# Sparse attention and gated FFN on one core: few large casting loads on one queue, values in 64-token rows, fewer casts

## The chip, the cores and the metric

One Trainium2 chip, one of its cores. The metric is device time in microseconds (us) of one execution. Most executions of a kernel agree closely; some ran at a lower granted TensorE clock and over 1.5% above the fastest run of their kernel. These are called slow here, and only fast runs enter a ratio. A profile is one execution. Stage times come from one profile per kernel and carry that uncertainty.

The engines: PE is TensorE (matmul), PEld its weight loads, DVE is VectorE, ACT is ScalarE, POOL is GpSimd, SP is SyncE. In the traces below VectorE, GpSimd and the matmuls of TensorE keep program order: where one of them waits, what stands behind it waits too.

## The reference

Attention of 4 batches, 8 heads, 768 tokens, 64 channels, followed by a gated FFN (512 to 1536 to 512). A token sees its neighbours within 15 positions, and 24 blocks of 32 tokens by one summary each (elementwise maximum of the keys, mean of the values).

```python
block, window = (32, 16)
k_sum = k.reshape(B, H, nb, block, D).max(axis=3)
v_sum = v.reshape(B, H, nb, block, D).mean(axis=3)
scores_l = scale * np.matmul(q, k.transpose(0, 1, 3, 2))
mask_l = np.abs(pos[:, None] - pos[None, :]) < window
scores_s = scale * np.einsum('bhsd,bhnd->bhsn', q, k_sum) + np.log(block)
a = softmax(concatenate([where(mask_l, scores_l, -1e9), scores_s]))      # shortened
attn = np.matmul(a, concatenate([v, v_sum]))
x = attn.transpose(0, 2, 1, 3).reshape(B * S, H * D)
return (1 / (1 + np.exp(-(x @ w_gate))) * (x @ w_val)) @ w_out
```

## The kernel before

For each tile of 64 queries the kernel multiplies one 120-row operand: 96 near tokens (64 and a halo of 16 on each side) and 24 block means. The values of a batch lie in one of two buffers `vx_t[0]`, `vx_t[1]`; batches alternate between them. Every part of these buffers that no load fills is set once, at the top of the program, ahead of all loads:

```python
vx_t = [const.tile([128, NQ, H, 66], BF16, name=f"vx{i}") for i in range(2)]
...
for t_ in vx_t:
    nc.vector.memset(t_[0:16, 0], 0.0)              # no token before the first
    nc.vector.memset(t_[64:96, NQ - 1], 0.0)
    nc.vector.memset(t_[:, :, :, 64:66], 1.0)       # the column that sums the weights
```

Values come through GpSimd's queue in one casting load (f32 in memory, bf16 in SBUF) per tile of 64 queries. Keys and queries of batches 0 and 1 come plain through the queues of SyncE and ScalarE and are cast by an engine. The opening, in program order:

```python
sk = [load_qk(k, 0, p, ...) for p in range(NP)]                     # SyncE queue
sq = [load_qk(q, 0, p, st, half=0, queue=nc.scalar) ...]            # ScalarE queue
load_v(0, 0, 3); make_masks(); load_v(0, 3, 6); make_zband(); load_v(0, 6, NQ)
for f0, nf in ((0, 1), (1, 1), (2, 2), (4, 2), (6, 2), (8, 2), (10, 2)):
    for wb, wap in ((wg_bf, moe_w_gate), (wv_bf, moe_w_val)):
        load_w(wb, wap, f0, nf)                                     # GpSimd queue
...                                                                 # attention of batch 0, first half
# q second half, w_out, keys and queries of batch 1 (cast on GpSimd), values of batch 1
```

The FFN works on half a batch (384 tokens) and one of 12 slices f of the hidden width at a time. The two products of an f, gate and value, come from one pool of four buffers.

```python
def m1(self, f, hf, c0=0, c1=NP):
    ...
    gp, vp = ps(...), ps(...)                        # four buffers in all
    # four matmuls into gp (gate), four into vp (value)
    nc.scalar.activation(out=gate, in_=gp, func=ACT.Tanh, scale=0.5)
    nc.vector.scalar_tensor_tensor(                  # hT, VectorE
        out=self.hT[hf][:, f, :], in0=gate, scalar=1.0, in1=vp, op0=ALU.add, op1=ALU.mult)
```

The softmax here doesn't subtract the row's maximum and nothing guards it: scores larger than these inputs give would overflow.

## Time and profile before

| | before |
|---|---|
| time, median of 3 runs | 255.56 us (253.16 to 256.45) |
| span of the profiled execution | 251.1 us |
| TensorE busy | 230.2 us, 92% |
| first full group of the FFN starts | 28.1 us |
| second half of batch 0's FFN starts | 49.5 us |

The page's slices cut the span in 40 parts; a digit is the busy share in tenths. A timeline lists start, length, engine, line and operation, and in brackets how long the engine had been idle and which event ended that. The lines of this page are shown in the prediction below. Busy time by stretch: the columns are the stretch, its length, then busy time and count of PE, PEld, DVE, ACT and POOL, then granted TensorE clock (1.00 is full), DMA share and GB/s.

```profile
28.10:49.50 21.40, 18.71 (x211) 11.36 (x209) 10.82 (x23) 12.04 (x24) 11.86 (x17) 1.00 1.22 270
```

This is the first half of batch 0's FFN: TensorE is busy for 18.71 of its 21.40 us, and the missing 2.69 are the wait for weights that the prediction shows.

### The profile page before, as it was taken

The page shows a single profiled execution, that of the slowest core. Times are in us where ns is not written, and L with a number is a line of the kernel's source. Part 1 is how long each engine was busy: PE and PEld are TensorE (multiplying, and loading weights), DVE is VectorE, ACT ScalarE, POOL GpSimd, SP SyncE. Part 2 cuts the span into 40 slices and gives each one's busy share as a digit, 9 for nine tenths or more (in the row PEclk, how much of TensorE's full clock was granted, in tenths as well). Part 3 has the DMA queues.
Part 4 walks back from the last instruction along what each step waited for, and adds up shares of the span by engine and source line. Part 5 has one row for each costly group of instructions (what it writes and reads, how often), then busy time and mean ns, then how long its engine had stood idle before and what let it go on. Part 6 is the DMA issues. An engine that isn't in the chain of part 4 may idle for free.

```text
span 251.1 us, 5090 instructions
## 1 busy us (share of the span) xinstructions
PE 230.2 (92%) x2020; PEld 130.3 (52%) x2032; DVE 119.2 (47%) x243; ACT 107.8 (43%) x193; POOL 111.7 (45%) x151
## 2 busy tenths in 40 slices
PE   1696899599999999799999999999999999999993
PEld 1473566366544556455554455555544465655441
DVE  5876348247833412976563208766543034444000
ACT  2862476239943344445631134645511243333121
POOL 8998276489998389994069930000000000000000
PEclk9999999999999999999999999999999999999999
DMA  6999999999999999999999965600024310000122
GB/s 220 238 158 162 226 270 287 263 189 142 124 122 170 225 221 145 193 171 206 176 121 163 197 171 132 113 13 3 0 76 147 117 42 0 4 0 0 57 112 84
DMA packets 100687, 34.27 MB, mean 136 GB/s; under 512 B 84496, under 2 KB 97208, under 8 KB 100280
## 3 DMA queue, kind: packets, MB, share of 16 engines
q0 software_dynamic: 70720, 12.46, 65.7%
q1 hardware_dynamic: 28856, 20.70, 33.5%
q10 hardware_dynamic: 1088, 0.79, 1.0%
q8 instruction: 16, 0.26, 0.4%
q14 instruction: 7, 0.06, 0.1%
HBM read 34.34 MB, written 6.29 MB: 162 GB/s over the span
## 4 chain that ended last, share of the span: by engine, by line
PE 71%; DMA 17%; POOL 6%; issue 2%; DVE 1%; ACT 1%; SPq 0%; POOLq 0%; ACTq 0%; DVEq 0%
PE m L414 22%; PE gp L397 21%; PE vp L397 21%; DMA wv<-in_moe_w_val_dram 11%; POOL vx L166 3%; DMA kTn<-nat 3%; PE sc L257 2%; PE av L340 2%; DMA vx<-vx 2%; PE vsp L280 1%; PE tp L197 1%; POOL wg L174 1%; DVE kTx L233 1%; PE br L368 1%; POOL wv L174 1%
## 5 line engine op out<-in xcount | busy, mean ns | idle before, releaser
L405 DVE SCALAR_TENSOR_TENSOR hT<-gate,vp 128x384 bf16<-128x384 f32 x96 | 52.8, 551 | 68.9 <-PE vp L397 65.0
L397 PE MATMUL vp<-xT,wv 128*128 128x384 bf16 x384 | 78.6, 326 | 4.2 <-DMA wv<-in_moe_w_val_dram 2.7
L397 PE MATMUL gp<-xT,wg 128*128 128x384 bf16 x384 | 78.8, 327 | 1.1 <-ACT xT L371 1.1
L404 ACT ACTIVATE gate<-gp 128x384 f32<-128x384 f32 x96 | 47.4, 494 | 51.4 <-DVE hT L405 42.9
L414 PE MATMUL m<-wo,hT 128*128 128x512 bf16 x276 | 64.3, 379 | 0.6
L397 PEld LDWEIGHTS <-wv 128*128 128x128 bf16 x384 | 37.5, 98 | 30.6 <-issue 3.1
L397 PEld LDWEIGHTS <-wg 128*128 128x128 bf16 x384 | 35.3, 98 | 22.1
L414 PEld LDWEIGHTS <-hT 128*128 128x128 bf16 x288 | 26.9, 98 | 30.7
L166 POOL DMA_DIRECT2D vx<-in_v_dram x48 | 37.0, 800 | 13.1 <-PE sc L257 9.0
L419 ACT ACTIVATE ot<-m 128x512 f32<-128x512 f32 x24 | 14.3, 597 | 52.1 <-PE m L414 51.9
L263 ACT ACTIVATE P<-sc 128x768 bf16<-128x768 f32 x32 | 26.0, 815 | 12.3 <-PE sc L257 12.2
L264 DVE TENSOR_TENSOR P<-P,mask 128x768 bf16<-128x768 bf16 x32 | 17.8, 555 | 14.1 <-ACT P L263 13.9
L311 POOL TENSOR_TENSOR vm<-vm 96x1024 f32<-96x1024 f32 (+4 forms) x20 | 20.4, 1020 | 5.8 <-DMA vm<-in_v_dram 4.4
L233 DVE TENSOR_REDUCE kTx<-kTn 128x24 bf16<-128x768 bf16 x16 | 15.2, 949 | 4.5 <-ACT kTn L203 2.5
L349 DVE TENSOR_TENSOR xs<-av,rec 128x768 bf16<-128x768 f32 (+1 forms) x20 | 15.9, 797 | 0.7
L197 PE MATMUL tp<-ident,qkbf 128*128 128x128 bf16 x96 | 8.9, 253 | 6.9 <-DVE qkbf L120 5.9
L257 PEld LDWEIGHTS <-kTx 64*128 64x128 bf16 x384 | 7.9, 97 | 11.8 <-issue 8.5
L347 DVE RECIPROCAL rec<-av 128x12 f32<-128x12 f32 (+1 forms) x20 | 4.3, 215 | 19.9 <-PE av L340 19.8
L257 PE MATMUL sc<-qT,kTx 64*128 64x64 bf16 x384 | 12.0, 196 | 1.9 <-DVE kTx L237 1.2
L156 POOL DMA_DIRECT2D nat<-in_q_dram x16 | 13.2, 894 | 0.4 <-issue 0.4
L122 POOL CAST qkbf<-nat 128x768 bf16<-128x768 f32 (+1 forms) x12 | 8.5, 723 | 11.0 <-DMA nat<-in_q_dram 7.6
L156 POOL DMA_DIRECT2D nat<-in_k_dram x16 | 13.3, 852 | 0.1
(50 smaller groups left out, 114.0 us busy)
## 6 DMA issues: line engine op xcount, KB each, us to landing
out_dram<-ot SPq DMA_DIRECT2D x24, 256.0 KB, 4.6
vx<-in_v_dram POOLq DMA_DIRECT2D x40, 96.0 KB, 5.4
vm<-in_v_dram SPq DMA_DIRECT2D x4, 768.0 KB
vm<-in_k_dram SPq DMA_DIRECT2D x4, 384.0 KB, 6.9
nat<-in_k_dram SPq DMA_DIRECT2D x4, 384.0 KB
nat<-in_q_dram SPq DMA_DIRECT2D x4, 384.0 KB, 13.9
wo<-in_moe_w_out_dram POOLq DMA_DIRECT2D x6, 256.0 KB, 16.2
nat<-in_k_dram POOLq DMA_DIRECT2D x16, 96.0 KB, 4.2
```

What stands on the lines that cost most here:

```text
L156: nc.gpsimd.dma_start(out=nat[:, h // 2, :, 64 * (h % 2):64 * (h % 2) + 64], in_=tap[b, h].rearrange("(c p) d -> p c d", p=128))
L166: nc.gpsimd.dma_start(out=vx_t[b % 2][r0:r0 + hi - lo, t, :, 0:64], in_=v[b, :, lo:hi, :].transpose([1, 0, 2]))
L233: nc.vector.tensor_reduce(out=kTx[:, 0, W:KX], in_=kTn[:, 16:16 + S].rearrange("p (n w) -> p n w", w=32), axis=AX.X, op=ALU.max)
L257: nc.tensor.matmul(out=sc[:, i, QT * t6:QT * (t6 + 1)], lhsT=kTx[64 * i:64 * i + 64, t, :], rhs=qT[64 * i:64 * i + 64, QT * t:QT * (t + 1) ...
L263: nc.scalar.activation(out=Ph, in_=sc[:, :, 0:6 * QT], func=ACT.Exp, scale=SCALE)
L264: nc.vector.tensor_tensor(out=Ph, in0=Ph, in1=mask[:, None, 6 * hf:6 * hf + 6, :].rearrange("p i t w -> p i (t w)") .to_broadcast([128, 2, ...
L311: nc.gpsimd.tensor_tensor(out=st[:, 0:n], in0=st[:, 0:n], in1=st[:, n:2 * n], op=ALU.add)
L349: nc.vector.tensor_tensor(out=xs[:, 0:3 * G].rearrange("p (g a) i d -> p g (a i) d", g=G), in0=avf[:, :, :, 0:64], in1=rec[:, 0:G].to_broa ...
L397: nc.tensor.matmul(out=o, lhsT=wb[:, c, 128 * f:128 * (f + 1)], rhs=self.xT[:, c, HALF * hf:HALF * (hf + 1)], start=(c == 0), stop=(c == N ...
L404: nc.scalar.activation(out=gate, in_=gp, func=ACT.Tanh, scale=0.5)
L405: nc.vector.scalar_tensor_tensor(out=self.hT[hf][:, f, :], in0=gate, scalar=1.0, in1=vp, op0=ALU.add, op1=ALU.mult)
L414: nc.tensor.matmul(out=self.m3, lhsT=self.hT[hf][:, f, 128 * tt:128 * (tt + 1)], rhs=wo_bf[:, f], start=(f == 0), stop=(f == NF - 1))
```

## The change

Its intent is to get batch 0's inputs and the weights in sooner, and to relieve engines of casts: few large casting loads, all on GpSimd's queue in one order; values in rows of 64 tokens, so that nothing is loaded twice, with VectorE copying the halo of 32 rows; no engine casts for batches 0 and 1; in the opening masks added through a matmul instead of multiplied in; in the opening near and mean products apart; later both halves of a score tile issued together. The core of the diff, cut (the rest is layout, masks and slot tables):

```diff
-    vx_t = [const.tile([128, NQ, H, 66], BF16, name=f"vx{i}") for i in range(2)]
+    vx_t = [const.tile([128, NU + 1, 66], BF16, name=f"vx{i}") for i in range(2)]
...
-    for t_ in vx_t:
-        nc.vector.memset(t_[0:16, 0], 0.0)
-        nc.vector.memset(t_[64:96, NQ - 1], 0.0)
-        nc.vector.memset(t_[:, :, :, 64:66], 1.0)
+    def clear_values(i):
+        t_ = vx_t[i]
+        nc.vector.memset(t_[0:W, :, 64:66], 1.0)
+        nc.vector.memset(t_[W:128, :, 64:66], 32.0)
+        nc.vector.memset(t_[0:16, 0, 0:64], 0.0)
...
+    def load_v(b, u0, u1, r0=0, r1=64):
+        nc.gpsimd.dma_start(
+            out=vx_t[b % 2][r0:r1, u0:u1, 0:64],
+            in_=rows_of(v[b, 0, 0:1], (QT * u0 - 16 + r0) * D, [[D, r1 - r0], [QT * D, u1 - u0], [1, D]]))
+    def load_values(b):
+        if b + 1 < B:
+            load_v(b, 0, NU + 1)
...
+        def halo(self, h0, h1, t0, t1):
+            nc.vector.tensor_copy(
+                out=self.heads(h0, h1, t0, t1, self.vx[64:96, 0:NU]),
+                in_=self.heads(h0, h1, t0, t1, self.vx[0:32, 1:NU + 1]))
...
+        def G(self, g, h=None):                      # block sums of batch 1, VectorE
+            nc.vector.tensor_reduce(out=sm, in_=st.rearrange("p (w d) -> p d w", w=32), axis=AX.X, op=ALU.add)
...
+    load_rows(k, 0, ...), load_rows(q, 0, ...)       # batch 0 (calls shortened)
+    load_v(0, 0, 1, 16, 64)
+    for p in range(NP):
+        load_v(0, 24 * p + 1, 24 * p + 25)
+    load_gates(...)                                  # all of gate and value weights
+    for h in (0, 4):
+        load_rows(k, 1, h, 4, 0, S, k1[:, h:h + 4])
+        load_rows(q, 1, h, 4, 0, S, q1[:, h:h + 4])
+    load_wo(0, 4)
+    load_wo(4, 4)
+    for g in range(2):
+        a1.L(g, queue=nc.gpsimd)
+    load_wo(8, 4)
+    load_values(1)
+    clear_keys(0)
...                                                  # masks, then attention of batch 0, first half
     f0.m1(0, 0, 3, 4)
+    more_masks()
+    clear_values(1)
...
+    NEXT = """
+        3 T0   4 T1   5 Z0   6 T2   7 Z1   8 T3   10 Z2   12 Z3 G0 M0   13 G1 M1   14 H0 H1   16 B0 B1
+        17 A0 A1   18 A2 A3 X0   19 X1   20 X2   21 X3"""
```

In the slot tables a number is a slot of the FFN and the letters are pieces of attention issued after it: T transposes, Q those of the second half's queries, E the key copies of that half, S scores of a half, Z of both, G or R block sums on VectorE or GpSimd, M their scaling and the move into the value buffer, H halo, B spread of the means, A value products, X output transposes.

## The prediction

> **What bounds the kernel now.** I read the page's busy rows first, then the slices, then the chain of waits in order of time, then the timelines of single engines.
>
> ```profile
> PE 230.2 (92%) x2020; PEld 130.3 (52%) x2032; DVE 119.2 (47%) x243; ACT 107.8 (43%) x193; POOL 111.7 (45%) x151
> ...
> PE   1696899599999999799999999999999999999993
> ...
> DMA  6999999999999999999999965600024310000122
> ```
>
> TensorE is the bound: 92% busy, and full from slice 9 on. Whatever is to be won lies in the first eight slices (50 us), in the slot after the last matmul, and in matmul work taken away. There the DMA row reads 9. The chain, in order of time, names what holds the opening (start us, length us, what):
>
> ```profile
> 13.72 0.74 POOL vx L166
> ...
> 25.31 21.82 DMA wv<-in_moe_w_val_dram
> ...
> 47.18 0.82 PE vp L397 x4
> ```
>
> and TensorE's timeline shows the one long pause of the FFN, with its releaser in brackets:
>
> ```profile
> 43.66 0.82 PE L397 MATMUL gp<-xT,wg 128*128 128x384 bf16 x4
> 47.18 0.82 PE L397 MATMUL vp<-xT,wv 128*128 128x384 bf16 x4 [2.69 <-DMA wv<-in_moe_w_val_dram]
> ```
>
> So the opening waits for transfers: values until 18.1 us (the block sums start then), the last weights until 47.1 us. The first half of the first FFN ends at 49.6 us by the chain. The rates, from busy time by stretch (last two columns DMA share and GB/s, which count the bytes written):
>
> ```profile
> 10.00:16.00 6.00, 5.39 (x66) 4.62 (x65) 5.29 (x11) 5.32 (x10) 5.72 (x9) 1.00 2.41 154
> ...
> 20.00:27.00 7.00, 4.51 (x69) 2.55 (x68) 4.84 (x13) 2.02 (x6) 4.91 (x7) 1.00 1.33 171
> ...
> 50.00:54.00 4.00, 4.00 (x26) 2.40 (x25) 1.76 (x4) 1.47 (x3) 3.12 (x5) 1.00 1.24 205
> ```
>
> The first is values alone (rows of 64 bf16), the second gate and value weights, the third the output weights: casting loads write 154, 171 and 205 GB/s, the more the longer the row.
>
> **What the Trainium skill says.** "DMA: Bandwidth & Descriptors", Specifications, gives about 358 GB/s of HBM for one core; a casting load reads twice what it writes, so 171 is 342 read (agrees), 205 is 410 (the trace is above it). The same page, "Issuing engines are not separate DMA queues": all transfers share 16 DMA engines; so moving batch 0's loads from the SP and ACT queues to GpSimd's gains no bandwidth. "TensorE: Matmul & The Clock Gate", Part 1, says that the VectorE queue is strict first in, first out; the trace agrees: the mask copies of 6.88 us stand behind two casts that waited for their loads, 0.86 us for the second, though they needed neither. "VectorE: DVE Perf Modes", the tier table, gives copies of bf16 in SBUF 4 elements a cycle: the 128x1152 key copy takes 0.45 us, which is that rate plus 0.15 us.
>
> **The change, part by part.**
>
> Casts go. Four pairs of key and query casts (0.55 us VectorE, 0.51 ScalarE) and 12 GpSimd casts leave; only the first 8 lay on the opening's path, some 0.5 us per pair. Against it, keys now come by the GpSimd queue: there the first packet moved only about 4.5 us after the first issue (the first value load, issued at 1.55 us, had done nothing by 6 us), while the plain loads had keys for a cast at 4.61 us. Even.
>
> Products. Block sums of batch 0 come by head pair (52 matmuls of 128 columns, not 12 of 512: 2.7 us, now pipelined with the value loads). Those of batch 1 go to VectorE and save 2.7 us of TensorE. Batch 1's transposes double in count (48 more at 55 ns: 2.6 us, or none if pairs overlap). Bias products add 8 x 0.16 = 1.3 us, but only in an opening that waits. Joined score halves save some 12 switches at 0.11 us (a group of four that follows a score group takes 0.76 us, else 0.65): 1.3 us.
>
> Values. A batch needs 64 x 97 rows, not about 96 x 96: a third fewer. The halo becomes two VectorE copies of 32x3168 per batch (825 ns at 4 a cycle + 0.15 = 1.0 us each), the spread of means two of 24x2904 (0.9 us): 3.8 us per batch, beside hT copies of 0.55 us in every 1.30 us. VectorE has room (47%), but in some slots it lags: 1 to 2 us per batch, 3 us in all.
>
> One GpSimd queue, in order, now carries everything. By bytes written and the rates above (keys and queries, 768-byte rows, between 171 and 205, taken as 190): keys and half the queries 1.18 MB, 6.2 us; values 0.79 MB at 154, 5.1; gate and value weights 3.15 MB at 171, 18.4; the other query half 0.39 MB, 2.3. From a first packet at 5 us the weights are in at 37.0 us, not 47.1. Ten microseconds: this is the gain that the change is made for. Behind them: keys and queries of batch 1, 1.57 MB, 8.3 us; output weights 1.57 MB at 205, 7.7; batch 1's values in f32 for the block sums, 1.57 MB, 7.9 us alone at about 0.2 MB a us but partly beside others, taken as 6; batch 1's values in bf16, 5.2. **These last land at 37.0 + 8.3 + 7.7 + 6 + 5.2 = 64 us.**
>
> Now the line that decides. The opening ends with clear_values(1), on VectorE, just before the FFN proper. Its third memset zeroes partitions 0 to 15 of unit 0 of the values of batch 1. The load of batch 1's values was issued earlier in the program and, unlike batch 0's, writes these very bytes (it starts at row 0, as there is a token before). A write after a write to the same bytes must wait. I built two instructions of no kernel to see it: a memset beside a load's columns carries no wait, one on its bytes waits for the load. VectorE runs in order, so from some 22 us, after hT of the first f, it stands until 64 us, and every hT stands behind it. The product tiles have four buffers, two pairs; TensorE can do f = 1 and 2, the gate product of f = 3, and stops at its value product at about 25 us. An idle of some 39 us, in place of a 2.7 us wait. Before, nothing like it: the memsets were put ahead of all loads.
>
> **The sum.** VectorE resumes at 64 us, hT takes 0.55, so the value product of f = 3 starts at 64.6. In the kernel before it started at 31.39 and the span ended at 251.08: 219.7 us of path. From these go the weight wait 2.7, batch 1's block sums 2.7, two query transposes already done in the idle 0.7, switches 1.3; to them come transposes 2.0, a colder TensorE clock after the idle 1.5 (its first transposes here took 0.11 us against 0.055 later), VectorE lag 3. That is 218.8, and a span of 283.4. Time stood 4.5 above span before (255.56 against 251.08): **288 us**, 13% slower.
>
> **Rivals.**
> First, no stall: if the memset waited for nothing, the weights at 37 us would end the first FFN half near 39.5 instead of 49.6; with 2.7 less of sums and 2 more of transposes the span is 241, the time 245, 4% faster. For it: the intent, and the DMA queue as today's limit. Against it: program order and the overlap of bytes, both plain in the source.
> Second, a wait for the same load elsewhere: without the memset, batch 1's halo copies and value products still need a load that lands at 64 us. But they come after the second half of the FFN, at about 61 to 67 us; a few us at most, inside the first rival: 247 to 250.
> Third, VectorE becomes the bound. It has 3.8 us more per batch, and block sums of batch 1 (two reductions of 96x2048, 1 element a cycle, 2.2 us each). For it: joined score halves give it bursts. Against it: over 50% idle now, 65 us of it waiting for value products. Up to 8 us: 293.
> Fourth, the queue is slower or faster than summed. At the skill's 358 GB/s the 20.4 MB read up to there take 57 us, landing 62; at this trace's 410, 50 and 55. If block rows and long descriptors hold up the ring, 70. So 279 to 294.
>
> **Range and chances.** The landing is worth -7 to +6, the work after it -4 to +5, mostly independent. 8 in 10: 279 to 297 us. The stall follows from the source; that I misread it, or that it is harmless, gets 7%, most of which is the first rival. Faster 0.05, same 0.02, slower 0.93.
>
> **What would show each step.** VectorE idle in one piece from about 22 to 64 us, its first instruction after it a memset of 16 partitions released by the DMA of batch 1's values. TensorE empty in the same time (five or six slices near 0), then full to the end. The chain of waits should hold one DMA item of some 39 us, by the name of the values, and gate and value weights should be gone from it. DMA should stay at 9 up to 64 us: weights in by 37, output weights by 53. After 65 us TensorE should need about 219 us to the end. I am wrong if that first memset waits for nothing, if the values land before 50 us, or if FFN stages after it run over 55 us a batch, for then VectorE was the bound.

## The result

| | before | after |
|---|---|---|
| time, median | 255.0 us of 4 runs (253.16 to 256.45) | 291.01 us of 4 runs (289.87 to 292.2) |
| ratio of fast runs | | 1.142, 95% interval 1.1328 to 1.1513 |
| span of the profiled execution | 251.1 us | 289.5 us |

A ratio is the mean time of one kernel's fast runs over that of the other's of the same rounds, so it is not quite the ratio of the medians. The predicted time was 288 us, its range 279 to 297: the change is slower by 14%, where 13% was predicted.

The page of the changed kernel, busy time and slices of 7.2 us:

```profile
PE 237.8 (82%) x2180; PEld 135.8 (47%) x2180; DVE 139.4 (48%) x270; ACT 106.9 (37%) x190; POOL 85.0 (29%) x102
...
PE   1989920003999999399999899999999999999994
...
DVE  6552200004964878951789853068974403444100
...
PEclk9965885555799999779999999999999999999999
DMA  6999999999909000275999999853000740000122
```

Slices 6 to 9 have three zeros of TensorE and four of VectorE (up to 65 us), while the DMA row reads 9: the engines stand, and a transfer runs. VectorE's timeline says which instruction stands, and TensorE's what that does:

```profile
33.68 0.22 DVE L91 MEMSET vx<- 96x194 bf16 x1
34.00 0.22 DVE L92 MEMSET vx<- 32x194 bf16 x1
68.63 0.09 DVE L93 MEMSET vx<- 16x32 uint32 x1 [34.40 <-DMA vx<-in_v_dram]
69.10 1.49 DVE L470 SCALAR_TENSOR_TENSOR hT<-gate,vp 128x384 bf16<-128x384 f32 x3 [0.39 <-issue]
```

```profile
32.11 0.81 PE L462 MATMUL gp<-xT,wg 128*128 128x384 bf16 x4
...
33.41 0.81 PE L462 MATMUL gp<-xT,wg 128*128 128x384 bf16 x4
...
35.26 0.82 PE L462 MATMUL gp<-xT,wg 128*128 128x384 bf16 x4
...
37.12 0.82 PE L462 MATMUL gp<-xT,wg 128*128 128x384 bf16 x4
69.71 1.44 PE L462 MATMUL vp<-xT,wv 128*128 128x384 bf16 x4 [31.77 <-DVE hT L470]
```

The three memsets are the three lines of `clear_values(1)`. The first two touch the columns 64 and 65 only and run at once. The third zeroes 16 partitions of the first 64 channels, which batch 1's load, issued earlier, also writes; it takes 0.09 us and is preceded by 34.40 us of nothing. Behind it stand the `hT` instructions from f = 1 on, and behind those TensorE, for 31.77 us. The four gate products shown are those of f = 1 to 4, so the value product at 69.71 us is that of f = 4. (The prediction, and the expectation of e1_order, call it f = 3.) The waits view adds up the same (engine, line, what it waited for: total, times, longest):

```profile
DVE vx L93 <- DMA vx<-in_v_dram: 34.4, 1, 34.4
PE vp L462 <- DVE hT L470: 32.5, 2, 31.8
```

The chain of waits is less helpful here. It has the idle as one item, but does not name the transfer:

```profile
34.22 34.39 issue
69.71 1.44 PE vp L462 x4
...
110.95 7.07 DVE sm L381 x2
118.06 1.91 DVE vx L324 x2
120.00 0.92 DVE vx L391
120.97 1.48 PE av L408 x24
```

A reader who looks at the chain alone sees "issue" and might look for slow dispatch. The memset's bracket in the timeline, or the waits view, gives the releaser. The last four items are a second place where VectorE now sets the end, at batch 1's values; it comes back below.

### The profile page after: what moved, and what is told of

Its sections match the earlier page's. It is cut to its first block, busy times and chain, and to the rows that moved or that the text cites. A ratio compares the mean times of both kernels' runs of the same rounds, so it can differ in the third digit from the quotient of the medians.

```text
span 289.5 us, 5322 instructions
## 1 busy us (share of the span) xinstructions
PE 237.8 (82%) x2180; PEld 135.8 (47%) x2180; DVE 139.4 (48%) x270; ACT 106.9 (37%) x190; POOL 85.0 (29%) x102
## 4 chain that ended last, share of the span: by engine, by line
PE 64%; issue 15%; DVE 12%; DMA 3%; ACT 3%; POOL 1%; SPq 1%; DVEq 0%; ACTq 0%; POOLq 0%
PE m L479 20%; PE vp L462 17%; PE gp L462 17%; PE av L408 3%; DVE hT L470 3%; DVE sm L381 2%; PE tp L203 2%; DVE P L288 2%; PE sc L280 2%; DMA k<-in_k_dram 2%; DMA kTn<-nat 2%; PE vsp L308 2%; DVE vx L324 1%; PE br L435 1%; ACT P L286 1%
## 5 line engine op out<-in xcount | busy, mean ns | idle before, releaser
L462 PE MATMUL vp<-xT,wv 128*128 128x384 bf16 x384 | 80.5, 332 | 32.5 <-DVE hT L470 32.5
L470 DVE SCALAR_TENSOR_TENSOR hT<-gate,vp 128x384 bf16<-128x384 f32 x96 | 51.9, 552 | 62.6 <-PE vp L462 60.1
L462 PE MATMUL gp<-xT,wg 128*128 128x384 bf16 x384 | 80.5, 331 | 1.2 <-ACT xT L438 0.6
L479 PE MATMUL m<-wo,hT 128*128 128x512 bf16 x288 | 65.8, 384 | 0.0
L479 PEld LDWEIGHTS <-hT 128*128 128x128 bf16 x288 | 27.8, 99 | 32.1 <-issue 1.1
L286 ACT ACTIVATE P<-sc 128x768 bf16<-128x768 f32 x32 | 24.5, 812 | 10.6 <-PE sc L280 10.6
L374 POOL TENSOR_TENSOR vm<-vm 96x1024 f32<-96x1024 f32 (+4 forms) x20 | 20.8, 1040 | 13.7 <-DMA vm<-in_v_dram 12.4
L288 DVE TENSOR_TENSOR P<-P,mask 128x768 bf16<-128x768 bf16 x28 | 16.9, 622 | 5.5 <-ACT P L286 4.4
L151 POOL DMA_DIRECT2D nat<-in_q_dram x16 | 14.6, 914 | 14.0 <-DMA vx<-in_v_dram 5.5
L158 POOL DMA_DIRECT2D vx<-in_v_dram x9 | 12.7, 1426 | 10.1 <-PE br L435 7.5
L417 DVE TENSOR_TENSOR xs<-av,rec 128x768 bf16<-128x768 f32 (+1 forms) x16 | 13.7, 858 | 0.7 <-DVE rec L415 0.2
L438 ACT COPY xT<-br 128x384 bf16<-128x384 bf16 (+1 forms) x12 | 6.9, 585 | 18.8 <-PE br L435 18.8
L408 PE MATMUL av<-vx,P 120*64 120x65 bf16 x336 | 8.4, 210 | 5.2 <-DVE vx L324 3.5
L408 PEld LDWEIGHTS <-P 120*64 120x64 bf16 x336 | 7.2, 124 | 9.2 <-issue 4.1
```

Of the source, the lines that this page charges most:

```text
L151: nc.gpsimd.dma_start(out=nat[:, h // 2, :, 64 * (h % 2):64 * (h % 2) + 64], in_=tap[b, h].rearrange("(c p) d -> p c d", p=128))
L286: nc.scalar.activation(out=Ph, in_=sc[:, :, 0:6 * QT], func=ACT.Exp, scale=SCALE)
L288: nc.vector.tensor_tensor(out=Ph, in0=Ph, in1=mask[:, None, 6 * hf:6 * hf + 6, :].rearrange("p i t w -> p i (t w)") .to_broadcast([128, 2, ...
L374: nc.gpsimd.tensor_tensor(out=st[:, 0:n], in0=st[:, 0:n], in1=st[:, n:2 * n], op=ALU.add)
L408: nc.tensor.matmul(out=av[r:r + 64, t // 6, (t % 6) // 2, i, 0:65], lhsT=P[0:KX, i, t, :], rhs=vx[0:KX, NQ * (2 * p + i) + t, 0:65], start ...
L417: nc.vector.tensor_tensor(out=xs[:, 0:3 * G].rearrange("p (g a) i d -> p g (a i) d", g=G), in0=avf[:, :, :, 0:64], in1=rec[:, 0:G].to_broa ...
```

## The experiments

All twelve runs gave correct results. **Theory**: the third memset waits for the last transfer on the queue, VectorE stands behind it, and that is the whole loss. **Rivals**: without that wait the kernel is faster than before, since weights come earlier (the first rival of the prediction, 245 us); or another wait for the same load, or VectorE, takes its place (the second and third). In the expectations "the base" is the kernel of e1_order. The stages of each kernel, read from the TensorE timeline of one profile, in us from the start:

| kernel | f=1 starts | second half starts | FFN batch 1 | batch 2 | batch 3 | span | profile's state |
|---|---|---|---|---|---|---|---|
| before | 28.1 | 49.5 | 94.0 | 148.0 | 200.3 | 251.1 | fast |
| after | 32.1 | 85.8 | 134.3 | 187.3 | 238.5 | 289.5 | fast |
| e1_order | 30.9 | 54.9 | 102.6 | 156.9 | 208.2 | 259.1 | slow |
| e2_nozero | 32.5 | 54.5 | 102.4 | 156.6 | 207.9 | 258.8 | fast |
| e3_early_load | 27.5 | 68.2 | 116.8 | 170.4 | 221.7 | 272.6 | fast |
| e4_sums_pool | 31.8 | 56.4 | 110.2 | 164.9 | 216.1 | 267.1 | slow |
| e5_warm | 28.8 | 49.2 | 100.7 | 155.6 | 206.9 | 257.8 | fast |
| e6_rest | 32.1 | 54.1 | 102.5 | 157.1 | 208.4 | 259.3 | fast |
| e7_sums_early | 32.4 | 54.1 | 99.6 | 157.5 | 208.8 | 259.7 | slow |
| e8_all | 32.4 | 52.3 | 93.3 | 151.2 | 202.5 | 253.4 | fast |
| e9_queue | 34.1 | 53.1 | 94.2 | 154.8 | 206.1 | 257.0 | slow |
| e10_again | 28.0 | 46.7 | 91.1 | 158.6 | 210.8 | 261.4 | unknown |
| e11_tensor_sums | 28.6 | 47.7 | 92.0 | 147.3 | 198.6 | 249.1 | fast |

### e1_order: the memsets of batch 1 ahead of its load

```diff
     load_wo(8, 4)
+    clear_values(1)
     load_values(1)
...
     more_masks()
-    clear_values(1)
```

> The changed kernel with the same work, one line moved: the memsets of batch 1's value buffer stand ahead of its load in the program. Theory (VectorE stood 34.4 us in order behind one memset that had to wait for the load): the wait is gone, the value product of f = 3 starts near 38 us instead of 69.7, the colder clock just after the idle goes too (some 2 us), so about 34 us less: 257 us, no better than the 255 of the kernel before. Rival (the halo copies and value products of batch 1 need that load anyway, so the wait only moves): at least 280 us, with a wait for the values of batch 1 elsewhere.

Measured 260.32 us median (256.59 to 260.87), ratio 1.018 to the kernel before (1.0091 to 1.0269, two fast runs). The 34-us wait is gone, and so are some 31 us. One moved line is worth almost all of the loss, but the kernel does not come out faster than before.

### e2_nozero: the third memset for batch 0 only

```diff
-        nc.vector.memset(t_[0:16, 0, 0:64], 0.0)
+        if i == 0:
+            nc.vector.memset(t_[0:16, 0, 0:64], 0.0)
```

> The changed kernel with only the third memset left out for batch 1's buffer (0.09 us of work; the result stays right, the load writes those bytes). Theory: as with the line moved, 257 us within 1%. If the two other memsets of that call, which stay where they were, also waited for the load, this would stay near 291 us and the moved line alone would help.

Measured 261.54 us median (260.61 to 264.46), ratio 1.033 (1.0261 to 1.0399). That is more than the 257 us within 1% that were expected, but far from the 291 of the rival. Here nothing else moves: the other two memsets stay behind the load in program order. VectorE in this kernel:

```profile
34.12 0.22 DVE L92 MEMSET vx<- 32x194 bf16 x1
35.33 0.56 DVE L471 SCALAR_TENSOR_TENSOR hT<-gate,vp 128x384 bf16<-128x384 f32 x1 [1.00 <-PE vp L463]
```

So it is not `clear_values` as such, nor its place after the load, but the 16 partitions of shared bytes alone. Zeroing them is needed for batch 0, whose load leaves these rows out; batch 1's load fills them.

### e3_early_load: the wait kept, its transfer moved forward

```diff
+    load_values(1)
     load_wo(0, 4)
     load_wo(4, 4)
     for g in range(2):
         a1.L(g, queue=nc.gpsimd)
     load_wo(8, 4)
-    load_values(1)
```

> The changed kernel with the memset left where it is and the load of batch 1's values moved ahead of the output weights and the block rows in the queue. Theory (the idle lasts until that load lands, wherever it stands in the queue): keys and queries of batch 1 were in at 44.5 us, the values take 5.2 us more, so VectorE resumes near 50 instead of 68.6 us: about 272 us. Rival (the idle lasts until the whole queue is drained, or has to do with the other loads): stays near 291 us.

Measured 274.7 us median (272.84 to 275.37), ratio 1.0817 (1.0771 to 1.0864). The memset's own view, first of the changed kernel and then of this one (duration min/median/max in ns, first and last start; below it what ended the idle):

```profile
L93 DVE MEMSET vx<- x2: 85/85/85, 6.6 to 68.6; 16x32 uint32 x2
...
  DMA vx<-in_v_dram: 34.4, 1
```

```profile
L93 DVE MEMSET vx<- x2: 85/85/85, 6.6 to 51.9; 16x32 uint32 x2
...
  DMA vx<-in_v_dram: 22.3, 1
```

The load lands 16.7 us earlier (51.9 against 68.6) and the span is 16.9 us shorter (272.6 against 289.5): one for one. The end hangs on that landing. This also settles how the prediction could be right without getting the start of the stall right.

### e4_sums_pool: block sums of batch 1 back on GpSimd (with e1_order)

The stage from the second half to batch 1's FFN takes about 48 us in after, e1_order and e2_nozero, against 44.5 before. In the changed kernel TensorE waits there for VectorE:

```profile
110.87 7.16 DVE L381 TENSOR_REDUCE sm<-vm 96x64 f32<-96x2048 f32 x2
```

```profile
119.09 0.25 PE L408 MATMUL av<-vx,P 120*64 120x65 bf16 x2 [3.53 <-DVE vx L324]
120.97 1.48 PE L408 MATMUL av<-vx,P 120*64 120x65 bf16 x46 [1.62 <-DVE vx L391]
```

Two block sums at 3.58 us each hold the halo copies (L324) and these hold the value products. The edit takes the sums from VectorE:

```diff
-    NEXT = "... 12 Z3 G0 M0   13 G1 M1   14 H0 H1   16 B0 B1 ..."
+    NEXT = "... 12 Z3 R0 M0   13 R1 M1   14 H0 H1   16 B0 B1 ..."
```

> As the run with the line moved, and batch 1's block sums on GpSimd (ten additions) instead of two reductions on VectorE. In the changed kernel these took 3.5 us each (7.1 together), the halo and mean copies stood behind them, and TensorE was empty from 115.5 to 121.0 us but for two products, then ran 5 us at half clock. Theory: some 5 to 7 us less than with the line moved alone, 250 to 252 us. Rival (the stage waits for something else there, such as the transfers of the means, or VectorE was not what held it): within 1 us of it.

Measured 268.54 us median (263.71 to 268.84), with one fast run only (263.71), so no ratio. A miss. GpSimd in this kernel (a slow profile):

```profile
69.12 0.82 POOL L151 DMA_DIRECT2D nat<-in_q_dram  x1 [5.77 <-DMA vx<-in_v_dram]
...
76.61 2.28 POOL L158 DMA_DIRECT2D vx<-in_v_dram  x1
78.84 5.97 POOL L374 TENSOR_TENSOR vm<-vm 96x1024 f32<-96x1024 f32 x5
```

GpSimd takes its instructions in order too. The 17 load issues for batch 2 stand ahead of the sums in the program, each issue waits its turn on the transfers, and the sums cannot start before 78.84 us. The stage grew to 53.8 us.

### e5_warm: filler matmuls in the opening (with e1_order)

In the changed kernel's opening the TensorE clock fell to half from 17.3 to 30.9 us. Some more small matmuls of no use are put between the block sums:

```diff
     a0.S(2, 0, True)
+    a0.warm(a0.vsp[:, 256:384], 16)
...
-    a0.sums(1)            # and sums(2, 4), sums(3, 4)
+    a0.sums(1, 6)         # and sums(2, 8), sums(3, 8)
```

> The run with the line moved (the base), and more filler matmuls in the opening: 16 in the 1.3 us in which TensorE waits after the third score group, 6, 8 and 8 ahead of the block sums. In the base and in the changed kernel the granted clock fell to half from 17 or 18 us for 14 us, and the first FFN group came at 30.9 to 32.5 us; in the run with the early load, of the same opening, it happened not to fall there, and the group came at 27.5. Theory (the clock falls as the opening's small matmuls leave TensorE too idle, and this costs 3 to 5 us): the clock stays full, the group comes at 27.5 to 28.5 us, and the time falls by 3 to 4 us against the base. Rival (the opening is set by the landings of the values and the hops between engines, the clock only follows): no gain, or the fillers' own 1 to 2 us lost.

Measured 260.78 us median (259.61 to 261.8), ratio 1.0274 (1.0231 to 1.0317): no gain. The stretch from 14 to 29 us in the kernel before, the changed kernel and this one:

```profile
14.00:29.00 15.00, 11.36 (x144) 7.18 (x143) 8.24 (x22) 5.71 (x13) 10.91 (x15) 1.00 1.60 176
```

```profile
14.00:29.00 15.00, 13.38 (x187) 10.03 (x185) 5.63 (x14) 4.79 (x10) 8.96 (x12) 0.61 2.23 175
```

```profile
14.00:29.00 15.00, 13.11 (x248) 9.53 (x243) 6.83 (x18) 6.24 (x14) 8.98 (x12) 1.00 2.21 174
```

The clock stayed full, the second half started at 49.2 us instead of some 54.7, and then the gain was lost in the next stage, which took 51.5 us instead of 48. Its VectorE:

```profile
74.34 7.18 DVE L381 TENSOR_REDUCE sm<-vm 96x64 f32<-96x2048 f32 x2
...
86.53 0.91 DVE L391 COPY vx<-vx 24x2904 bf16<-24x2904 bf16 x1 [3.08 <-DMA vx<-mb]
89.04 0.91 DVE L391 COPY vx<-vx 24x2904 bf16<-24x2904 bf16 x1 [1.60 <-DMA vx<-mb]
```

After the same two sums, the copies that spread the means waited for the small transfers that bring them; TensorE stood 7.6 us there and its clock was half from 82 to 92 us. The second limit swallows what the first gives.

### e6_rest: the second score halves issued apart (on the changed kernel with e1_order)

```diff
-        1 Q0 Q1   2 E0 E1 Q2 Q3   3 S0b S1b   4 E2 E3   5 S2b S3b
+        1 Q0 Q1 E0 E1   2 Q2 Q3 E2 E3   3 S0b   4 S1b   5 S2b   6 S3b
```

The key copies (E) also come one or two slots earlier.

> The base, with the second half of batch 0's attention spread: keys spread two slots earlier, score halves one per slot and not two. In the base this stage took 24.0 us from the first FFN group to the second half of the FFN, against 18.7 in the kernel before without its weight wait; TensorE stood 2.6 us behind a key copy on VectorE, with two masks, a halo copy and an hT ahead of it, and the clock then fell for 3.4 us. Theory (a burst on VectorE is what TensorE waits for): 20 to 21 us there, 3 to 4 us less in all than the base. Rival (the work is the same, and the burst only moves): within 1 us.

Measured 259.99 us median (257.86 to 261.1), ratio 1.0235 (1.0174 to 1.0295). The stage took 22.0 us, as in e2_nozero, and 24.0 in e1_order's slow profile (there one key copy of 128x576, at 41.86 us, took 1.71 us while GpSimd spent 2.27 us on issuing batch 1's values; the next such copy took 0.30). The time doesn't tell it from e1_order. Inconclusive, and small in any case.

### e7_sums_early: block sums on GpSimd, ahead of batch 2's loads (with e1_order)

```diff
-        3 T0   4 T1   5 Z0   6 T2   7 Z1   8 T3   10 Z2   12 Z3 G0 M0   13 G1 M1   14 H0 H1   16 B0 B1
+        3 T0   4 T1   5 Z0 R0 M0   6 T2   7 Z1 R1 M1   8 T3   10 Z2   12 Z3   14 H0 H1   16 B0 B1
```

> The base, with batch 1's block sums on GpSimd as in the run that made it slower, but issued ahead of batch 2's loads on GpSimd, not behind them. There GpSimd stood in order behind the loads of batch 2 until 78.9 us, and the means came at 96.3 instead of 89.1. Theory (it was the order on GpSimd, not the engine): sums start when the block rows are in, near 55 us, end near 66, and nothing waits for means; batch 0's second half, with batch 1's attention, takes 41 to 42 us instead of 47.7: 5 to 6 us less than the base. Rival (the loads of batch 2 come later in exchange, and the first keys of batch 2 wait for them): gain under 2 us, with a longer wait for the transposed keys.

Measured 257.73 us median (254.21 to 261.53), ratio 1.0059 (0.9992 to 1.0125) from two fast runs. The median is 2.6 us below e1_order's, where 5 to 6 were expected. By the two kernels' slow profiles the stage fell from 47.7 to 45.5 us, but batch 1's FFN, where batch 2's attention runs, grew from 54.3 to 57.9: now the loads of batch 2 stand behind the sums. GpSimd's order is a resource, and each of the two uses pays for the other.

### e8_all: e1_order, e5_warm, e6_rest and e7_sums_early together

The edit is the sum of the four shown.

> The base with all three: filler matmuls, spread second half, sums on GpSimd ahead of the loads. If the three losses are separate: some 12 us less than the base, 246 to 248 us, 2 to 3% faster than the kernel before, which is near the 245 us of the prediction's first rival. If they share one cause, or if the gain of the earlier weights is not there: 250 to 255.

Measured 254.1 us median (253.1 to 255.16), ratio 1.0013 (0.997 to 1.0057): the time of the kernel before, and the lesser of the two outcomes expected. The stage to batch 1's FFN took 41.0 us, shorter than before's 44.5, and batch 1's FFN gave it back with 57.9 against 54.0:

```profile
102.71 0.95 DVE L240 TENSOR_REDUCE kTx<-kTn 128x24 bf16<-128x768 bf16 x1 [4.64 <-DMA kTn<-nat]
```

```profile
105.15 1.37 PE L462 MATMUL vp<-xT,wv 128*128 128x384 bf16 x4 [4.49 <-DVE hT L470]
```

This is the opening's pattern in small: VectorE, in order, waits 4.64 us for keys of batch 2 that came late, and TensorE 4.49 us for the `hT` behind it.

### e9_queue: block rows and values ahead of the output weights (on e8_all)

```diff
-    load_wo(0, 4)
-    load_wo(4, 4)
     for g in range(2):
         a1.L(g, queue=nc.gpsimd)
-    load_wo(8, 4)
+    clear_values(1)
     load_values(1)
+    load_wo(0, 4)
+    load_wo(4, 4)
+    load_wo(8, 4)
```

(with fillers of 20, 8, 12 and 12 instead of 16, 6, 8 and 8)

> The run with all three, and the queue reordered: block rows and values of batch 1 ahead of the output weights, 20, 8, 12 and 12 fillers instead of 16, 6, 8 and 8. There batch 2's loads stood on GpSimd behind sums that waited for the block rows until 56 us, and the first keys of batch 2 were transposed only at 102.7 us, which cost the FFN of batch 1 some 4 us against the kernel before (57.9 against 54.0 us); the opening lost its clock at 23.3 us. Theory: block rows land near 50, sums end near 62, batch 2's loads follow at once; that FFN takes 54 to 55 us and the first group comes at 29 us: 248 to 250 us, 1.5 to 2.5% faster than the kernel before. Rival (output weights, now last in the queue, land after 70 us and hold the second products; or the opening stays at half clock): 252 to 256.

Measured 255.7 us median (252.79 to 259.79), ratio 1.0037 (0.9947 to 1.0126). A miss. In its profile, a slow one, the clock fell at 22.7 us in spite of more fillers, and GpSimd waited 25.4 us in all for the block rows. What makes the clock fall in the opening therefore stays open: fewer fillers kept it full in e5_warm, and in e8_all, with the same fillers as e5_warm, it was half for 10.2 us from 23.3 us on. In e3_early_load, with the changed kernel's opening and no added fillers, it was 1.00 from 14 to 29 us, and f = 1 started at 27.5 us. So no run shows that the fillers keep the clock up.

### e10_weights and e10_again: the kernel before, weights alone earlier

The question that is left is why earlier weights, the reason of the change, are worth so little. So the kernel before gets them earlier with nothing else of the change: batch 1's keys and queries go behind the weights on GpSimd's queue, where they no longer compete.

```diff
+    held = []
+    for p in range(NP):
+        st = staging(6)
+        held.append((load_qk(k, 1, p, st[0], queue=nc.gpsimd), load_qk(q, 1, p, st[1], queue=nc.gpsimd)))
     for i in range(6):
         load_wo(i)
     for p in range(NP):
-        st = staging(6)
-        s_ = (load_qk(k, 1, p, st[0]), load_qk(q, 1, p, st[1]))
-        srcs[1][p] = [cast_qk(s_[0], "pool"), cast_qk(s_[1], "pool")]
+        srcs[1][p] = [cast_qk(held[p][0], "pool"), cast_qk(held[p][1], "pool")]
```

> The kernel before, with one thing of the change alone: gate and value weights earlier. Keys and queries of batch 1 leave the queue that runs beside the weights and go behind them (1.57 MB read twice in f32, some 8 us of transfer). The question is what earlier weights are worth. Theory (TensorE waited 2.69 us for them in all, the rest of the 22 us that the chain of waits gives the last weights lay beside work): weights land near 38 to 40 instead of 47.1 us, that wait is gone, and the time falls by 2 to 3 us, about 1%; less if batch 1's first keys now come late. Rival (the prediction's side estimate: the first half of the FFN ends with the weights, so ten microseconds earlier are worth ten): 245 to 247 us.

Measured: fast runs 256.59 to 259.69 us, ratio 1.0178 (1.0094 to 1.0263). A miss: 2 to 3 us less than the kernel before was expected. Its profile fell in a slow run of 279.94 us at a mean clock of 0.848, so the same kernel was looked at again:

> The same kernel as the run with the weights alone earlier; its profile fell in a state with the clock at 0.85 throughout, where TensorE shows no wait for weights, while its fast runs were 1.8% slower than the kernel before. One more look for a profile in a fast state. Theory (the 2.7 us are won, and lost again because keys, queries and later loads of batch 1 come later): first half of the FFN about 18.7 us after its first group, and more time than the kernel before's 44.5 us from there to the FFN of batch 1. Rival (the opening itself is slower): the first group later than 28.1 us by the whole loss of 3 to 4 us.

263.11 us, one run at a mean clock of 0.974, above every fast run of this kernel; what this profile loses late is more than a fast run loses. The first half of batch 0's FFN, and later VectorE in batch 1's FFN:

```profile
28.00:46.70 18.70, 18.69 (x211) 11.45 (x209) 10.82 (x23) 12.09 (x24) 10.69 (x16) 1.00 1.18 280
```

```profile
117.94 0.95 DVE L233 TENSOR_REDUCE kTx<-kTn 128x24 bf16<-128x768 bf16 x1 [6.83 <-DMA kTn<-nat]
```

TensorE needs 18.69 us of work in this stage, against 18.71 in the kernel before. With the wait gone the stage takes 18.70 us instead of 21.40. So earlier weights are worth 2.7 us, because TensorE had work for all but 2.7 us of the 21.82-us chain item. This kernel is still slower in the end. In this profile batch 1's FFN took 67.5 us instead of 54.0, with VectorE waiting for batch 2's keys as shown; that GpSimd's fuller queue made them late is argued and not tested.

### e11_tensor_sums: block sums of batch 1 on TensorE (on e8_all)

The sums go where neither VectorE nor GpSimd is asked, by head pair as batch 0's are, and batch 1's f32 block rows are not loaded any more:

```diff
-    for g in range(2):
-        a1.L(g, queue=nc.gpsimd)
...
+        def U(self, p, h=None):
+            self.sums(p)                 # 13 matmuls of 128 columns
+            self.means(p)                # ScalarE
+        def W(self, *_):
+            nc.vector.tensor_copy(
+                out=self.heads(0, H, 0, NQ, self.vx[96:120, 0:NU, 0:64]),
+                in_=vs[96:120, :, None].to_broadcast([NS, H, NQ, 64]))
...
-        ... 5 Z0 R0 M0   6 T2   7 Z1 R1 M1   8 T3   10 Z2   12 Z3   14 H0 H1   16 B0 B1
+        ... 5 Z0   6 T2   7 Z1   8 T3   10 Z2   12 Z3 U0 U1   13 U2 U3 H0   14 H1 W
```

> The run with all three, but batch 1's block sums on TensorE again, by head pair as those of batch 0: 52 matmuls of 128 columns (2.9 us) and one spread copy on VectorE, in exchange for 1.57 MB of block rows, ten GpSimd additions and the wait of batch 2's loads behind them. Theory (GpSimd's place in order was what cost the FFN of batch 1 4 us): batch 2's keys are in before they are needed, that FFN takes 54 instead of 57.9 us, TensorE has 2.9 us more: 252 to 254 us. Rival (the late first keys come from elsewhere): 256 to 258.

Measured 252.54 us median (251.36 to 256.47; fast runs 251.36, 251.37 and 253.72), ratio 0.9931 (0.9846 to 1.0017). The best of all, and by the interval still the same as before. Its page:

```profile
PE 230.9 (93%) x2249; PEld 133.8 (54%) x2262; DVE 131.8 (53%) x267; ACT 107.9 (43%) x194; POOL 82.0 (33%) x98
...
PE   1698899999999999989989999999999999999994
```

TensorE is busy 230.9 us, within 1 us of the kernel before's 230.2, and at 93% there is little idle left to take. No version beat the kernel before by 2%.

## Why the prediction was right

**The step that decides.** The third memset waits for the load of batch 1's values; this is shown by its releaser in the trace, by e2_nozero (take these 16 partitions away, and the wait is gone) and by e3_early_load (move the landing by 16.7 us, and the end moves by 16.9). The four-buffer argument was right in kind and wrong by one f: TensorE stopped at the value product of f = 4, not 3. ScalarE had read the gate products of f = 1 to 3 and so freed their buffers; three value products and the gate product of f = 4 fill four.

**The landing.** Predicted 64 us, measured 68.6. Weights were in at 36.8 us (predicted 37.0) and batch 1's keys and queries at 44.8 (by the sum 45.3), each from its issue and time to landing. That these two agree is partly luck: the sum let the first packet move at 5 us, but by then the first load had landed (issued at 1.46, in at 5.05), so the transfers started sooner and ran slower than summed. The term that was mis-sized is the rest: output weights and block rows took 17.4 us instead of 13.7, the values 6.3 instead of 5.2.

**The start of the stall.** Predicted some 22 us for VectorE and 25 for TensorE, measured 34.2 and 37.9; the idle of TensorE was 31.8 us, not 39. The opening was slower than thought and than before, with the clock at half from 17.3 to 30.9 us. It cost nothing, as the end was set by the landing.

**The path behind it.** From that value product to the end: predicted 218.8, measured 289.5 - 69.7 = 219.8 us, against 219.7 in the kernel before. That these agree is partly luck: 218.8 and 219.7 count from f = 3, 219.8 from f = 4. In the kernel before the value product of f = 4 starts at 33.02 us, so like for like the path was 218.1 us, and grew by 1.7 where the prediction let it shrink by 0.9. By the stage table: up to the second half 16.1 us against 16.5; to batch 1's FFN 48.5 against 44.5; the three FFNs 53.0, 51.2 and 51.0 against 54.0, 52.3 and 50.8. Ahead of the second half the removed weight wait of 2.7 us is nearly all lost again: TensorE's clock averaged 0.52 from 69.71 to 75.61 us, by estimate some 2.8 us lost (5.9 us x 0.48), where 1.5 was predicted. The 4 us lost after it fit the two waits for VectorE shown under e4_sums_pool (3.53 and 1.62 us), since a block sum took 3.58 us, not 2.2; the runs that took the sums off VectorE changed other things too, so the share of each is not shown.

**The last term.** I added 4.5 us between span and time, from a median and a profile of different executions. The changed kernel's profiled run took 291.26 us with a span of 289.5: 1.8. So 5.1 us too little by the landing, 1.0 by the path and 2.7 too much here make the 291 against 288: errors that partly cancel.

**What was wrong beside the main line.** The first rival, "the weights at 37 us would end the first FFN half near 39.5 ... the time 245", fell. Without the stall the kernel takes 257 to 264 us (fast runs of e1_order and e2_nozero, medians 260 and 262). The step that failed is taking ten microseconds off the chain: the item of 21.82 us named the weights, but TensorE worked through all but 2.7 us of it (e10_again). In e2_nozero's profile 7.7 us then come on top of before's 251.1: 4.4 until f = 1, 0.6 until the second half, 3.4 until batch 1's FFN, and -0.7 after that. With a full clock in the opening f = 1 started 3 to 5 us earlier (27.5 us in e3_early_load, 28.8 in e5_warm), no sooner than the kernel before's 28.1 by more than 0.6 us. With the block sums off VectorE the stage to batch 1's FFN took 41.0 us (e8_all) and 44.3 (e11_tensor_sums). The third rival, VectorE as the bound, thus holds for one stage, and the second for none: in e2_nozero that load did not hold TensorE up. The chain was to name the values' DMA; it said "issue".

## What to carry to other kernels

Before moving an initialisation, list who else writes those bytes and where that writer stands: an instruction of 0.09 us behind a load that was queued last stops an in-order engine, and through it the bound engine, until that load and all that is queued ahead of it have landed. Set constant parts ahead of the loads, or only in the buffer that needs them. And the length of a chain item is not what its removal gives; the idle time of the bound engine that it ends is (2.7 of 21.8 us here). When work is moved to one in-order queue, as here to GpSimd, its order has to be planned like a buffer: what is put first delays all the rest.

## What the Trainium skill lacked or had wrong

- "TensorE: Matmul & The Clock Gate", Part 1, ties a falling clock to an idle window, and in a second case to short idles between groups of matmuls, without saying how much of these is enough. Here the changed kernel's TensorE is listed busy 2.15 us from 13.9 to 17.3 us, and then its clock fell to half; the kernel before is listed busy 0.72 us from 44.00 to 47.41 us and kept 1.00. Why is open; listed busy time alone doesn't tell, as far as these runs show.
- "DMA: Bandwidth & Descriptors", Specifications: some 358 GB/s from HBM for one core, without a condition. The kernel before's casting loads of the output weights wrote 205 GB/s, which is 410 read. The page isn't contradicted: further down, under its measured bandwidths, it gives 358 for the case that both cores of a pair stream, and here one core ran. The prediction used the bare row.
- The same page, "Anatomy of one DMA", says that many descriptors can be issued before the cost shows. Issuing the one load of a batch's values (6208 rows of 64) held GpSimd for 2.27 us, against some 0.8 us for a head's keys or queries (768 rows). From e2_nozero:

```profile
41.27 2.27 POOL L159 DMA_DIRECT2D vx<-in_v_dram  x1 [1.10 <-DMA nat<-in_q_dram]
```

- "VectorE: DVE Perf Modes", the tier table, gives tensor_reduce one element a cycle. The key maximum over contiguous elements agrees (128x768 in 0.95 us); the block sum of 96x2048, read with a stride of 64 f32 elements, took 3.58 us instead of the 2.2 that I had estimated from that rate. The table has no entry for a stride; "SBUF — State Buffer" says that reads which cross to a new line pay a penalty, but not how much. That the stride is the reason was not tested here.
- No page says how the profile names a wait of this kind: the timeline and the waits view gave the transfer (34.40 us), the chain of waits called the same time "issue" (34.39 us).
